# Paired one-hots, a moved register read and a moved seam between two expert layers

## The chip, the core and the metric

One NeuronCore of a Trainium2 chip runs the whole program. The metric is the device time of one execution in microseconds (us). The engines are TensorE (PE, with its weight loads as PEld), VectorE (DVE), ScalarE (ACT), GpSimd (POOL) and SyncE (SP), which here only issues transfers and reads registers for them. Each engine takes its instructions in order and waits at semaphores for the others.

## The reference

```python
# attention: (4, 8, 576, 64); heads 0-3 a window of 32, heads 4-7 a dilated one
x = attention(q, k, v)                # 2304 tokens x 512
def moe(x, w_gate, w1, w2, ...):      # twice, 8 experts, D=512, F=1024
    logits = x @ w_gate               # layer 2: + modality_bias[modality_id]
    e_idx = argmax(logits, axis=1)    # one expert for each token
    gate = softmax(logits)[e_idx]     # layer 1: times sigmoid(x @ w_output_gate)[e_idx]
    for e in range(8):
        out[e_idx == e] = gate * (relu(x[e_idx == e] @ w1[e]) @ w2[e])
```

The second layer takes the first one's output.

## The kernel before

All of it lies in one function, and the order of the instructions is written out by hand. The attention runs first (lines 283 to 656). Each expert layer then works on **slots** of 128 tokens, up to 27 of them (`NSLOT`), at least 18 (`NMIN`); from slot 18 on each lies in an `If` nested in the one before (L1019), and the number of slots `nsl` is read from the table `tab` into a register of every engine by `values_load` (L1018) behind slot 2 (`KE - 1`). Products are made in split 16-bit: a weight is a high part (`hi_piece`, L100, ScalarE) and a low part (`lo_piece`, L105, VectorE), both from the 32-bit `raw` that SyncE loads (L92) in eight pieces of 512 KB. `splits` takes a list such as `B8:12 D8:12`: split these pieces, then load the next expert's into their place.

A slot (`slot`, L946 on) gathers its tokens (POOL, L886), turns them (by DMA, L893, or on TensorE, L901), and makes two products. The first (`mm1`, L923) runs in two halves of 48 matmuls of 128 columns; each half ends in a relu by ScalarE (`hh`, L933) and its remainder by VectorE (`hl`, L934). The second (L997) has 24 matmuls of 512 columns, first over `hh`, the last eight over `hl`. Its result goes through `Post1.out` (ScalarE L1133, VectorE L1134) to 16-bit rows `y`, is written to DRAM, turned on TensorE (L1152) and by VectorE out of PSUM (L1153), and multiplied with the second router (`router`, L1161); VectorE adds the logits (L1170). The router's PSUM tile `plg` is a single one.

Other work is put between by **hooks**: `at(s, k, ...)` names a slot and a point in it. The points follow each other as 0 (ahead of the first half), 8 (behind 8 of its matmuls), 1 (behind 32), 2 (behind the half), then its relu, 3, 4 (behind 32 of the second half), the second relu, 5, then 9, 6, 10 (behind 4, 12, 20 matmuls of the second product) and 7 (behind it).

`sort` (L701 to 872) is such work, cut in steps: from the logits it makes each token's expert, by a scan and two matmuls its place, then two one-hots (its slot, `ob`, L806, L807; its row, `A`, L812), from which matmuls make the index (`pidx`, L817) and the gates (`pg`, L863). `table` makes `tab` and after it slot 3's weights are asked for. `first_slots` (L224 to 277) does the same for the two slots that a layer begins with: in the attention's tail for layer 1 and in slots 15 to 17 for layer 2. In slots 0 to 2 the first expert's weights serve; slot 3's are split by `FIRST[0]` to `FIRST[3]` from hook (1, 6) on. Slots 0 and 1 of layer 1 keep their results in PSUM (`pya`) until slot 2's hook (2, 5), where `first_out` brings them out; at (2, 7) they are turned.

The last slot of layer 1 has its rows made, turned and put through the router by layer 2's first hooks (`out(None)`, L1129, L1130; `router(None)`, L1167, L1168), and the sort of layer 2 (`so2`) begins behind that.

## Time and profile before

| | us |
|---|---|
| median of 3 runs (643.93 to 645.22) | 644.5 |
| the profiled execution | 644.33 |
| its span, first to last instruction | 642.6 |
| TensorE busy | 590.8 (92%) |
| VectorE busy | 366.6 (57%) |
| ScalarE busy | 272.9 (42%) |
| POOL busy | 191.4 (30%) |

The attention fills the first 152 us, layer 1 follows to 425 and layer 2 to 634. A matmul's end is modelled, so matmuls overlap in the records, and a busy share near one only says that TensorE was never seen idle. An idle time in brackets stands ahead of the instruction that ended it, with the engine or transfer whose signal came last. "issue" is time in which nothing visible was waited for. Register reads and branches are not counted as busy.

### The profile page before, as it was taken

To read this page: it belongs to the slowest core of one execution; us is meant where nothing else is said; L and a number is where in the kernel's file an instruction comes from. 1 tells how busy PE (TensorE), PEld (TensorE's weight loads), DVE (VectorE), ACT (ScalarE), POOL (GpSimd) and SP (SyncE) were. 2 spreads that over 40 slices of the span, in tenths; PEclk is the share of its full clock that TensorE was granted. 3 is DMA by queue.
4 is the path that set the end of the run, shared out by engine and by line. 5 is a ranking of instruction groups with operands and counts; after the bars stand their busy time and mean duration, and the time that the engine had idled before them with its cause. 6 is when DMAs were issued, how large, how long until landed. Compare 5 with 4: busy or idle time off the path is not lost. (4 is left out here: it accounts for less than half of the span.)

```text
span 642.6 us, 19352 instructions
## 1 busy us (share of the span) xinstructions
PE 590.8 (92%) x7380; PEld 456.6 (71%) x7380; DVE 366.6 (57%) x653; ACT 272.9 (42%) x370; POOL 191.4 (30%) x305
## 2 busy tenths in 40 slices
PE   3879788977989999999999999989999999999994
PEld 2768677977667767777686686866776777777772
DVE  6798888788888436953848922249541101013460
ACT  5767666772185115923626611111532111114550
POOL 2657767613132310001110410002553212212220
PEclk9889999866999999999999999999999999999998
DMA  8864759872399765995967872220994514133921
GB/s 285 258 202 165 232 173 298 268 160 71 119 378 328 226 119 151 357 298 140 236 222 205 204 165 56 57 32 18 307 331 135 103 51 101 53 99 95 306 63 37
DMA packets 100864, 114.15 MB, mean 178 GB/s; under 512 B 64399, under 2 KB 69263, under 8 KB 100752
## 3 DMA queue, kind: packets, MB, share of 16 engines
q1 hardware_dynamic: 95072, 94.89, 51.8%
q0 software_dynamic: 5280, 17.13, 8.7%
q8 instruction: 59, 0.97, 0.6%
q10 hardware_dynamic: 400, 0.72, 0.3%
q14 instruction: 53, 0.43, 0.2%
HBM read 209.13 MB, written 18.22 MB: 354 GB/s over the span
## 5 line engine op out<-in xcount | busy, mean ns | idle before, releaser
L923 PEld LDWEIGHTS <-wb 128*128 128x128 f16 x4032 | 229.4, 98 | 8.6 <-issue 3.6
L923 PE MATMUL ph<-xT,wb 128*128 128x128 f16 x3648 | 210.7, 219 | 2.2 <-DMA xT<-xg 1.1
L934 DVE SCALAR_TENSOR_TENSOR hl<-ph,hh 128x512 f16<-128x512 f32 x84 | 57.7, 689 | 164.3 <-ACTq L942 145.2
L997 PE MATMUL py<-wb,hh 128*128 128x512 f16 x608 | 137.9, 379 | 1.8 <-ACT hh L933 1.8
L997 PEld LDWEIGHTS <-hh 128*128 128x128 f16 x672 | 63.5, 98 | 71.5 <-ACT hh L933 2.7
L933 ACT ACTIVATE hh<-ph 128x512 f16<-128x512 f32 x84 | 50.2, 597 | 150.9 <-PE ph L923 145.3
L105 DVE SCALAR_TENSOR_TENSOR wb<-raw,wb 128x1024 f16<-128x1024 f32 (+1 forms) x80 | 104.6, 1346 | 13.2 <-ACT wb L100 11.8
L100 ACT ACTIVATE wb<-raw 128x1024 f16<-128x1024 f32 (+1 forms) x80 | 87.2, 1135 | 8.1 <-ACTq L942 4.1
L997 PE MATMUL py<-wb,hl 128*128 128x512 f16 x304 | 71.8, 379 | 0.0
L997 PEld LDWEIGHTS <-hl 128*128 128x128 f16 x336 | 32.8, 98 | 40.2 <-DVE hl L934 0.9
L1263 POOL DMA_INDIRECT out<-y,idx x16 | 16.2, 1011 | 99.0 <-ACTq L942 80.7
L447 PE MATMUL po<-v,pT 128*96 128x65 f32 x384 | 41.2, 260 | 0.1
L447 PEld LDWEIGHTS po<-v,pT 128*96 128x96 f32 x384 | 37.9, 176 | 0.2 <-DVE xh L454 0.2
L386 PE MATMUL ps<-kk,qs 128*96 128x128 f16 x192 | 30.4, 231 | 4.5 <-DVE qs L370 2.1
L886 POOL DMA_INDIRECT xg<-x_dram,idxaa x23 | 25.4, 1103 | 29.7 <-DMA xT<-xg 18.6
L386 PE MATMUL ps<-kk,ql 128*96 128x128 f16 x192 | 30.6, 232 | 3.7 <-DVE ql L364 3.7
L431 PE MATMUL pst<-mt,msel 128*128 128x96 bf16 x192 | 30.1, 217 | 4.0 <-ACT mt L420 4.0
L434 ACT ACTIVATE pT<-pst 128x384 f32<-128x384 f32 x48 | 23.5, 490 | 22.8 <-PE pst L433 22.1
L387 DVE TENSOR_REDUCE M<-ps 96x4 f32<-96x512 f32 x48 | 31.6, 681 | 2.6 <-PE ps L386 2.1
L1262 ACT ACTIVATE y<-py,gsb 128x512 f32<-128x512 f32 x16 | 11.0, 686 | 51.2 <-PE py L997 48.3
L386 PEld LDWEIGHTS <-ql 128*96 128x96 f16 x192 | 23.9, 132 | 12.2 <-DVE ql L364 5.4
L386 PEld LDWEIGHTS <-qs 128*96 128x96 f16 x192 | 24.2, 131 | 9.6 <-issue 4.1
(401 smaller groups left out, 727.7 us busy)
## 6 DMA issues: line engine op xcount, KB each, us to landing
raw<-in_w1a SPq DMA_DIRECT2D x95, 512.0 KB
raw<-in_w2a SPq DMA_DIRECT2D x92, 512.0 KB
raw<-in_w1b SPq DMA_DIRECT2D x75, 512.0 KB
raw<-in_w2b SPq DMA_DIRECT2D x72, 512.0 KB
qk<-in_qk SPq DMA_DIRECT2D x16, 608.0 KB
v<-in_vw SPq DMA_DIRECT2D x16, 390.0 KB
y_dram<-y SPq DMA_DIRECT2D x11, 260.0 KB
y_dram<-lotmp SPq DMA_DIRECT2D x10, 260.0 KB
```

Source lines behind the costliest of these rows:

```text
L100: nc.scalar.activation(wb[:, 0, s], raw[:, s], AF.Copy, scale=SW)
L105: nc.vector.scalar_tensor_tensor(out=wb[:, 1, s], in0=raw[:, s], scalar=SW, in1=wb[:, 0, s], op0=ALU.mult, op1=ALU.subtract)
L386: nc.tensor.matmul(ps[:, j, :], q[:, h, QT * i:QT * i + QT], kk[:, h, QT * i:QT * i + 128], start=False, stop=w == 1 and j == 3, skip_grou ...
L387: nc.vector.tensor_reduce(out=Ms[n][:, 4 * g:4 * g + 4], in_=ps, axis=AX.X, op=ALU.max)
L431: nc.tensor.matmul(ps[:, j, :], msel[:, typ, j, :], mt[:, g, :], start=j == 0, stop=False, skip_group_check=True)
L434: nc.scalar.activation(pTs[n][:, 4 * g:4 * g + 4, :], ps, AF.Exp, scale=0.125 / (SQK * SQK))
L447: nc.tensor.matmul(po[:, h, i, :], pT[:, NQ * h + i, :], v[:, h, i, :], start=True, stop=True)
L886: nc.gpsimd.indirect_dma_start(t, None, src, bass.IndirectOffsetOnAxis(start.idx[:, s:s + 1], 0))
L923: nc.tensor.matmul(ph[:, j, :], w[:, c, fs], xT[:, parts[c + i], :], start=k == 0, stop=k == 47, skip_group_check=True)
L933: nc.scalar.activation(hs, ph, AF.Relu)
L934: nc.vector.scalar_tensor_tensor(out=hl[:, 4 * g:4 * g + 4, :], in0=ph, scalar=0.0, in1=hs, op0=ALU.max, op1=ALU.subtract)
L997: nc.tensor.matmul(to, a, w, start=k == 0, stop=k == len(ops) - 1)
```

## The change

Six edits. (1) One-hots are compared in pairs: the index of each token is copied twice, side by side, as 16-bit values (`pp2`, `pr2`), and `one_hot` compares it with two neighbouring columns at a time; the slots' one-hots get a 28th column (`NSP`) so that their number is even, and all operands are 16-bit. (2) The sort keeps `eq` by expert, so that the 16-bit `oh` is written in a row instead of in strides; two passes read in strides instead. (3) The third and fourth split of slot 3's weights go behind the first half of slot 2 and behind its second. (4) The read of the number of slots goes from behind slot 2 to behind 20 matmuls of its second product. In slot 17 the router product of slot 15 goes from ahead of the second half to behind 4 matmuls of the second product. (5) In layer 2's slot 0 the turn of layer 1's last rows goes from ahead of the first half to behind 32 of its matmuls, router and sort's first step behind the half, the sort's second step behind 4 matmuls of the second product. (6) The hint ahead of each branch on `nsl` is also given to VectorE.

The allocations of `Bg`, `obp`, `pidx` and `pg` grow from `NSLOT` to `NSP` columns; their readers take the first 27.

```diff
@@
+NSP = 28
+HINT = [mybir.EngineType.PE, mybir.EngineType.DVE]
@@
-    tokv = const.tile([P, NSLOT], F16, name="tokv")
+    tokv2 = const.tile([P, NSLOT, 2], F16, name="tokv2")
+    tokv = tokv2[:, :, 0]
...
+    def one_hot(out, vals, pairs):
+        n, m = out.shape[1], out.shape[2] // 2
+        sh = [P, n, m, 2]
+        nc.vector.tensor_tensor(out.rearrange("p t (j k) -> p t j k", k=2),
+                                vals.rearrange("p (j k) -> p j k", k=2).unsqueeze(1).to_broadcast(sh),
+                                pairs.unsqueeze(2).to_broadcast(sh), op=ALU.is_equal)
@@ first_slots
+        pp2 = T("fp2", [-1, 2], F16)
+        v.tensor_copy(pp2, pi[:, 2].unsqueeze(2).to_broadcast([P, n, 2]))
...
-            v.tensor_tensor(A[:, a:e], iota_row.unsqueeze(1).to_broadcast([P, e - a, P]), pi[:, 2, a:e].unsqueeze(2).to_broadcast([P, e - a, P]), op=ALU.is_equal)
+            one_hot(A[:, a:e], iota_row, pp2[:, a:e])
@@ sort
-        eq = T("eq", [-1, E])
-        v.tensor_tensor(eq, lg, mxb, op=ALU.is_equal)
-        v.tensor_tensor(eq, eq, desc.unsqueeze(1).to_broadcast(sh), op=ALU.mult)
+        eq, st = T("eq", [E, -1]), [P, E, nt]
+        v.tensor_tensor(eq, lg.rearrange("p t e -> p e t"), mx.unsqueeze(1).to_broadcast(st), op=ALU.is_equal)
+        v.tensor_tensor(eq, eq, desc.unsqueeze(2).to_broadcast(st), op=ALU.mult)
         mi, mb = T("mi", [-1]), T("mb", [-1])
-        v.tensor_reduce(out=mi, in_=eq, axis=AX.X, op=ALU.max)
+        v.tensor_reduce(out=mi, in_=eq.rearrange("p e t -> p t e"), axis=AX.X, op=ALU.max)
...
-        v.tensor_tensor(oh.rearrange("p e t -> p t e"), eq, mb.unsqueeze(2).to_broadcast(sh), op=ALU.is_equal)
+        v.tensor_tensor(oh, eq, mb.unsqueeze(1).to_broadcast(st), op=ALU.is_equal)
...
+        bmh = T("bmh", [NSP], F16)
+        gp.memset(bmh[:, NSLOT:], 0.0)
         gp.tensor_scalar(bm, s_even, h, 1000.0, op0=ALU.is_ge, op1=ALU.mult)
-        gp.tensor_tensor(bm, bm, bs, op=ALU.add)
+        gp.tensor_tensor(bmh[:, :NSLOT], bm, bs, op=ALU.add)
...
+        pr2 = T("pr2", [2, -1, 2], F16)
+        v.tensor_copy(pr2, pi[:, 1:3].unsqueeze(3).to_broadcast([P, 2, nt, 2]))
...
-        v.tensor_tensor(ob, bm.unsqueeze(1).to_broadcast(sb), pi[:, 1].unsqueeze(2).to_broadcast(sb), op=ALU.is_equal)
-        v.tensor_tensor(obp, ob, tokv[:, :nt].unsqueeze(2).to_broadcast(sb), op=ALU.mult)
+        one_hot(ob, bmh, pr2[:, 0])
+        s4 = [P, nt, NSP // 2, 2]
+        v.tensor_tensor(obp.rearrange("p t (j k) -> p t j k", k=2), ob.rearrange("p t (j k) -> p t j k", k=2),
+                        tokv2[:, :nt].unsqueeze(2).to_broadcast(s4), op=ALU.mult)
...
-            v.tensor_tensor(A[:, a:a + n], iota_row.unsqueeze(1).to_broadcast([P, n, P]),
-                            pi[:, 2, a:a + n].unsqueeze(2).to_broadcast([P, n, P]), op=ALU.is_equal)
+            one_hot(A[:, a:a + n], iota_row, pr2[:, 1, a:a + n])
@@ slot
-                tc.mark_branch_hint_location(f"{start.name}{s + 1}", hint=nsl > s + 1, engines=PE)
+                tc.mark_branch_hint_location(f"{start.name}{s + 1}", hint=nsl > s + 1, engines=HINT)
...
-            if s == NMIN - 1:
-                post.router(s - 2)
...
                 if k == 4:
                     hook(9)
+                    if s == NMIN - 1:
+                        post.router(s - 2)
...
                 if k == 20:
                     hook(10)
+                    if s == KE - 1:
+                        count()
...
+        def count():
+            nonlocal nsl
+            nsl = nc.values_load(tab[0:1, 0, 31:32], min_val=1, max_val=NSLOT)
+
         for s in range(NMIN):
             slot(s, nsl)
-            if s == KE - 1:
-                nsl = nc.values_load(tab[0:1, 0, 31:32], min_val=1, max_val=NSLOT)
@@ plan of layer 1
-    at(2, 0, lambda: gt.memset(y16p[1][:, 2 * DM:], 0.0), lambda: start1.first_splits(FIRST[2]))
+    at(2, 0, lambda: gt.memset(y16p[1][:, 2 * DM:], 0.0))
     at(2, 1, lambda: start1.turned(KA + 1))
     at(2, 2, run(so1))
-    at(2, 3, lambda: start1.first_splits(FIRST[3]))
+    at(2, 3, lambda: start1.first_splits(FIRST[2]))
+    at(2, 5, lambda: start1.first_splits(FIRST[3]))
@@ plan of layer 2
-    at(0, 0, lambda: post1.out(None, py1), lambda: post1.transposes(None))
-    at(0, 8, lambda: post1.router(None), run(so2))
-    at(0, 5, run(so2))
+    at(0, 0, lambda: post1.out(None, py1))
+    at(0, 1, lambda: post1.transposes(None))
+    at(0, 2, lambda: post1.router(None), run(so2))
+    at(0, 9, run(so2))
```

## Rows read from the trace of the kernel before

**Rows 1.** Busy time by stage: start:end, length, each engine's busy us (count), clock, DMA share, GB/s.
```profile
180.00:200.00 20.00, 17.09 (x237) 13.69 (x235) 16.16 (x15) 14.96 (x17) 8.44 (x14) 1.00 1.05 358
...
197.00:213.50 16.50, 16.15 (x234) 13.20 (x232) 15.64 (x32) 6.57 (x9) 1.44 (x2) 1.00 1.05 356
...
340.00:370.00 30.00, 28.77 (x362) 20.92 (x360) 28.19 (x41) 19.91 (x24) 7.76 (x9) 1.00 0.74 203
...
420.00:460.00 40.00, 36.67 (x447) 26.76 (x445) 24.78 (x68) 7.78 (x12) 11.00 (x18) 1.00 0.28 91
460.00:634.00 174.00, 173.59 (x1963) 125.89 (x1961) 50.51 (x54) 53.42 (x72) 47.43 (x63) 1.00 0.48 137
```

**Rows 2.** Timeline of TensorE: start, length, operation, count, [idle before it <- what ended it].
```profile
163.05 1.90 PE L997 MATMUL pya<-wb,hl 128*128 128x512 f16 x8 [0.29 <-DVE hl L934]
...
167.31 0.59 PE L997 MATMUL pya<-wb,hh 128*128 128x512 f16 x2 [0.30 <-DVE wb L105]
...
182.72 1.27 PE L863 MATMUL pg<-Bga,Aa 128*128 128x135 f16 x18
...
188.05 1.90 PE L997 MATMUL py<-wb,hh 128*128 128x512 f16 x8 [1.38 <-ACT hh L933]
...
195.99 2.84 PE L923 MATMUL ph<-xT,wb 128*128 128x128 f16 x48 [1.14 <-DMA xT<-xg]
...
213.54 0.61 PE L1152 MATMUL pyt<-identh,y 128*128 128x128 f16 x8 [0.39 <-DVE fe_meb L196]
...
359.78 0.44 PE L1161 MATMUL plg<-wr2h,yT 128*128 128x8 f16 x12 [1.23 <-DVE lg L1170]
...
426.77 0.40 PE L1152 MATMUL pyt<-identh,y 128*128 128x128 f16 x4 [1.50 <-ACT y L1129]
```

**Rows 3.** Groups of VectorE's instructions by shape: count | busy us, mean ns | idle before.
```profile
L1153 DVE COPY yT<-pyt 128x1024 f16<-128x1024 f16 x22 | 15.0, 681 | 0.9 <-PE pyt L1152 0.9
...
L370 DVE COPY qs<-qs 64x1152 f16<-64x1152 f16 x15 | 6.8, 451 | 0.2
...
L812 DVE TENSOR_TENSOR Ab<-c16t,pib 128x1152 f16<-128x1152 f16 x3 | 3.9, 1352 | 0.0
...
L724 DVE TENSOR_TENSOR ohb<-eqb,mbb 128x216 f16<-128x216 f32 x1 | 1.1, 1128 | 0.0
...
L759 DVE TENSOR_REDUCE posb<-psb 128x27 f32<-128x216 f32 x1 | 0.5, 544 | 0.0
...
L718 DVE TENSOR_REDUCE mib<-eqb 128x27 f32<-128x216 f32 x1 | 0.4, 378 | 0.0
```

**Rows 4.** Timeline, the attention's last stage, VectorE behind the first one-hot.
```profile
144.53 0.17 DVE L451 TENSOR_SCALAR rc<-po 96x12 f32<-96x12 f32 x1 [0.74 <-PE po L447]
```

**Rows 5.** Timelines of ScalarE and of VectorE, slot 2 of layer 1.
```profile
184.51 1.91 ACT L100 ACTIVATE wb<-raw 128x2048 f16<-128x2048 f32 x1 [1.46 <-DMA raw<-in_w2a]
...
187.38 0.61 ACT L933 ACTIVATE hh<-ph 128x512 f16<-128x512 f32 x1
...
189.82 2.29 DVE L105 SCALAR_TENSOR_TENSOR wb<-raw,wb 128x2048 f16<-128x2048 f32 x1 [0.48 <-ACT wb L100]
...
193.29 0.74 DVE L1134 SCALAR_TENSOR_TENSOR xgA<-pya,gsa,xgA 128x512 f16<-128x512 f32 x1
```

**Rows 6.** Instructions of line 1018, TensorE's: ns min/median/max, first and last start us.
```profile
L1018 PEldq TENSOR_LOAD <-tab x2: 402/634/865, 195.1 to 461.8; - x2
```

**Rows 7.** Timeline of VectorE, slot 17 of layer 1.
```profile
364.79 3.52 DVE L105 SCALAR_TENSOR_TENSOR wb<-raw,wb 128x1024 f16<-128x1024 f32 x3
```

**Rows 8.** Timeline, ScalarE and VectorE where layer 2 begins.
```profile
426.03 0.69 ACT L1129 ACTIVATE y<-py,prg 128x512 f16<-128x512 f32 x1 [6.04 <-SPq L1019]
...
429.23 0.24 DVE L1167 TENSOR_TENSOR lgt<-plg,eqlaa 128x80 f32<-128x80 f32 x1 [0.55 <-PE plg L1161]
...
433.19 0.61 DVE L727 TENSOR_TENSOR_SCAN incb<-mask,ohb 128x216 f16<-128x216 f16 x1
...
441.44 3.89 DVE L812 TENSOR_TENSOR Ab<-c16t,pib 128x1152 f16<-128x1152 f16 x3
```

More of the change, by code (lines that the diff above doesn't have):

```diff
@@ L162, in slot_consts @@
         v.memset(s_odd[:, 1:2], 0.0)
-    tokv = const.tile([P, NSLOT], F16, name="tokv")
+    tokv2 = const.tile([P, NSLOT, 2], F16, name="tokv2")
+    tokv = tokv2[:, :, 0]
     def token_values():
-        nc.vector.tensor_scalar(tokv, blk128, iota_p, -TOK0, op0=ALU.add, op1=ALU.add)
+        nc.vector.tensor_scalar(tokv2, blk128.unsqueeze(2).to_broadcast([P, NSLOT, 2]), iota_p, -TOK0, op0=ALU.add, op1=ALU.add)
     zt = const.tile([P, ROW], F16, name="zt")
@@ L800, in table @@
             start.eql, start.nlast = eql, nlast
-        sb = [P, nt, NSLOT]
+        sb = [P, nt, NSP]
         nf = 3 + len(extra)
-        Bg = T("Bg", [-1, 1 + nf, NSLOT], F16)
-        ob, obp = Bg[:, :, 0], T("obp", [-1, NSLOT], F16)
-        v.tensor_tensor(ob, bm.unsqueeze(1).to_broadcast(sb), pi[:, 1].unsqueeze(2).to_broadcast(sb), op=ALU.is_equal)
-        v.tensor_tensor(obp, ob, tokv[:, :nt].unsqueeze(2).to_broadcast(sb), op=ALU.mult)
+        Bg = T("Bg", [-1, 1 + nf, NSP], F16)
+        ob, obp = Bg[:, :, 0], T("obp", [-1, NSP], F16)
+        one_hot(ob, bmh, pr2[:, 0])
+        s4 = [P, nt, NSP // 2, 2]
+        v.tensor_tensor(obp.rearrange("p t (j k) -> p t j k", k=2), ob.rearrange("p t (j k) -> p t j k", k=2),
+                        tokv2[:, :nt].unsqueeze(2).to_broadcast(s4), op=ALU.mult)
         yield
@@ L811, in sort @@
             n = min(ACH, nt - a)
-            v.tensor_tensor(A[:, a:a + n], iota_row.unsqueeze(1).to_broadcast([P, n, P]),
-                            pi[:, 2, a:a + n].unsqueeze(2).to_broadcast([P, n, P]), op=ALU.is_equal)
+            one_hot(A[:, a:a + n], iota_row, pr2[:, 1, a:a + n])
         yield
-        px = pp.tile([P, NSLOT], F32, name="pidx", tag="pyt")
+        px = pp.tile([P, NSP], F32, name="pidx", tag="pyt")
         for t in range(nt):
@@ L820, in sort @@
         idxf = T("idxf", [NSLOT])
-        v.tensor_scalar(idx, px, TOK0, None, op0=ALU.add)
-        act.activation(idxf, px, AF.Copy, bias=TOK0)
+        v.tensor_scalar(idx, px[:, :NSLOT], TOK0, None, op0=ALU.add)
+        act.activation(idxf, px[:, :NSLOT], AF.Copy, bias=TOK0)
         start.idx, start.idxf = idx, idxf
@@ L835, in sort @@
             so, sg = T("so", [-1, E]), T("sg", [-1])
-            v.tensor_tensor(so, eq, mi.unsqueeze(2).to_broadcast(sh), op=ALU.is_equal)
+            v.tensor_tensor(so, eq.rearrange("p e t -> p t e"), mi.unsqueeze(2).to_broadcast(sh), op=ALU.is_equal)
             v.tensor_tensor(so, og, so, op=ALU.mult)
@@ L859, in sort @@
         yield
-        pg = pp.tile([P, 1 + nf, NSLOT], F32, name="pg", tag="plg")
+        pg = pp.tile([P, 1 + nf, NSP], F32, name="pg", tag="plg")
         for t in range(nt):
@@ L864, in sort @@
         fl = m1.tile([P, 1 + nf, NSLOT], F32, name=f"fl{nm}")
-        act.copy(fl, pg)
+        act.copy(fl, pg[:, :, :NSLOT])
         g = m1.tile([P, NSLOT], F32, name=f"gs{nm}")
```

## The prediction

> **What bounds the kernel now.** I read the busy time by stage first, then TensorE's timeline with its gaps, then for each gap the engine that ended it. From 460 us to the end TensorE is busy for 173.59 of 174 us [rows 1]: nothing in that stretch can be won by moving work, it only starts earlier or later. The granted clock is 1.00 there and in all the stretches the change touches [rows 1]. So the change is worth what it takes out of the gaps, and those are few: about 3 us in 180 to 200, 1.2 us in 340 to 370, 3.3 us in 420 to 460 [rows 1]. Each has its place: in layer 1's slot 0 the second product waits for VectorE (0.29 and 0.30 us), in slot 2 for ScalarE (1.38), at the start of slot 3 (1.14), in slot 4 (0.39), in slot 17 (1.23), and at the seam of the layers (1.50 in its largest piece) [rows 2]. The second thing to see is VectorE: 28.19 of 30 us busy in 340 to 370 [rows 1]. Where it is that full, a TensorE gap that goes is replaced by a wait for VectorE, and the gain is VectorE's shift, not the gap's length.
>
> The profiled execution took 644.33 us (span 642.6, 1.7 around it), 0.17 under the median of 644.5. I sum against 644.33 and add 0.17 at the end.
>
> **One-hots in pairs.** Before, every one-hot is a product of a row with one element repeated; 1152 elements take 1352 ns [rows 3]. No row shows a two-source operation over 16-bit pairs, so its price is bounded: below by the copy of 1152 16-bit elements, 451 ns, above by the 1352 ns of now [rows 3]. I take the copy of 1024 16-bit elements out of PSUM, 681 ns, which cannot use the fastest form either: 681 x 1152/1024 = 0.77 us a piece, and at the same pace 0.50 us for the 756 elements of a slot one-hot in layer 2 and 0.34 for the 504 in layer 1 (before, at 1352/1152, 0.86 and 0.57). The Trainium skill's VectorE: DVE Perf Modes (What auto-detection actually checks) says that a two-source operation handles two elements a cycle if all its tensors are 16-bit with a step of 1; by its 0.96 GHz a piece would be 0.60 us plus the fixed part (estimate), so the sum would be the one I take; no run so far shows such an operation.
>
> The transposed one-hot of the sort writes 16-bit elements in strides and takes 1128 ns for 216; contiguous I price it like the contiguous pass over 216 elements, 378 ns [rows 3]. In exchange two passes now read in strides; the row of such a read is 544 against 378 ns [rows 3], so plus 0.17 each. Net for layer 2's sort: 1.13 - 0.38 - 0.34 = 0.41 us shorter; for layer 1's 144 elements two thirds, 0.3. Each sort also gets one small cast, some 0.2 us.
>
> In **slot 0 of layer 1** VectorE saves 0.3 - 0.2 + 2 x 0.23 (slot one-hots) + 2 x 0.58 (row one-hots) = 1.7 us before the index is out. TensorE's waits of 0.29 and 0.30 go, with a smaller one between; the index, the table and so the request for slot 3's weights come about 1.1 us earlier (0.6 to 1.3).
>
> The same one-hot in the attention's tail (1664 elements) saves nothing: the next VectorE operation waits 0.74 us for TensorE anyway [rows 4]. The 28th column adds 27 elements to a slot's products in layer 2, 0.03 us each at 1352/1152 ns an element, four or five of them per layer; they lie beside the big product's matmuls, and uncovered would cost 0.15 us.
>
> **The splits of slot 2.** Now ScalarE's third split sits ahead of the first relu: it waits 1.46 us for its weights at 184.51, runs 1.91, and the relu comes at 187.38 [rows 5]; TensorE's 1.38 us is that. After, the relu runs as soon as the copy of the 18 gate matmuls is out, which end at 184.0 now [rows 2] and 1 us earlier then, so at 183.5 to 184, and the split behind it: at 184.0 to 184.5, limited by its data, not later than now. So TensorE's second product starts when its first is done, 3 us earlier. But at its end it needs the two rows of results of slots 0 and 1, and those VectorE makes last: the fourth low split (189.82, 2.29 us), then y and y of slot 1, ending at 194.03 [rows 5]. In the new order VectorE does: first low part of hl at 184.5, third low split 185.9 to 188.2, second hl to 188.9, fourth low split to 191.2, the two y to 192.6: 1.4 us earlier than now, 0.95 if the weights came no earlier. Of the moved loads on SyncE's queue the first pair (2 x 512 KB) now goes behind the slot's transposing DMA instead of ahead of it and is issued with the third low split's end, within 0.5 us of now; the second pair with the fourth's, earlier. The transposing DMA itself no longer sits behind them.
>
> **The register read.** TensorE's read of the slot count takes 402 and 865 ns in the two layers [rows 6]. The long one is the 1.14 us gap in front of slot 3 [rows 2]. In layer 2 the short one, at 461.8, costs nothing: TensorE shows no gap there [rows 1], it works on the matmuls queued ahead of it. Four matmuls from the end of a product, with 12 or more of 0.2 us in the queue, the first is covered too; if that cover were gone the price is the gap it makes now. On VectorE, POOL, ScalarE and SyncE it is 0.3 to 0.5 us, ahead of work that waits longer for something else.
>
> **Layer 1's start in sum.** TensorE alone would reach slot 3 2.8 us earlier. VectorE, busy for all but a trace of 197 to 213.5 [rows 1], reaches its first split there 1.75 to 2.7 us earlier (its y 1.4, plus what the turn and the register reads no longer queue). In slot 4 TensorE already waits 0.39 us for it [rows 2], so VectorE's shift decides: -2.1 us, from -1.2 to -2.7. The transfers are at their limit there too (share 1.05 [rows 1]); each load is let go by a low split, so they shift with VectorE.
>
> **The router product.** At 359.78 TensorE waits 1.23 us because the bank of logits is single and its last reader, on VectorE, comes late [rows 2]. Moved into the second product, the router finds it free. But its own reader now stands behind the three splits at 364.79, which end at 368.3 [rows 7], and the next router product, at the slot's end, needs the bank again. VectorE is about 0.7 us earlier by then (two pieces of 640 elements and one of 384 at nearly half price, less one cast) and 0.3 by hl no longer waiting: 367.3. TensorE would be there at 367.1 (from 359.78 - 1.23 on, 3.1 for 48 matmuls and the transposes, 5.1 for 24 wide ones, 0.3 for the moved router). It waits some 0.4: gain 0.8, from 0 to 1.23.
>
> **The seam.** Now: y by ScalarE at 426.03, the transposes 1.50 us late, the copy, the router, then the sort from 429.23 to 433.80, and its first matmul follows at once, with no product of slot 0's second half done [rows 2, 8]. After, TensorE starts the first product as soon as its branch is through, about 425.95, as the other engines do now [rows 8]. 32 matmuls (2.84 us for 48, the last one's tail of some 0.15 off: 0.056 us apart [rows 2]) take it to 427.7; y is done at 427.5 and hides. Transposes, copy, router: 429.55, so the sort begins 0.3 later than now, is 0.41 shorter, and ends at 433.7. TensorE reaches the sort's matmuls after four of the second product at 432.95 and waits 0.85 us. By then it has done four matmuls (0.85 us) that it now does afterwards, and it goes on 0.15 us earlier: gain 1.0, from 0.6 to 1.4. The row one-hots (3.89 us from 441.44 [rows 8]) come to 2.3 and end 1.7 us ahead of the index matmuls, so they don't wait.
>
> **Hints for VectorE.** No row shows one on VectorE. In the late slots VectorE waits for TensorE most of the time (it is busy for 50.51 of 174 us in layer 2's [rows 1]), so the instructions themselves cost nothing. At the seam all engines go through the last branch between 425.27, where TensorE's wait of 1.50 us begins, and 426.03 [rows 2, 8]; if VectorE were the last one through, a branch fetched ahead could give back some of these 0.76 us, and if the hint fetched the wrong way it could cost as much. I take 0, the near end, since ScalarE's wait there was ended by SyncE's branch and not VectorE's [rows 8].
>
> **Sum.** 2.1 + 0.8 + 1.0 = 3.9 us: 644.33 - 3.9 + 0.17 = 640.6; I write 640.5.
>
> **Rivals.** (1) The pairs run at the old pace, so only reorderings count. Then the weights come no earlier (-1.2 us in layer 1), the router's reader is late (-0.1), and the row one-hots end after TensorE has reached the index matmuls, which eats all but 0.1 of the seam: 643.1. For it: no row shows the pair form; against: the copies of 16-bit data in rows 3. Chance 0.1. (2) VectorE's queue takes back one of the two smaller gains (the router's reader behind three splits, or the sort as the limit at the seam): 641.5. For it: VectorE is full at both places. Chance 0.14. (3) Slower: runs of two elements are handled like the strided 16-bit write of 1128 ns for 216 elements, 5.2 ns each. Then a piece of 1152 takes 6 us, three of them in layer 2 alone hold the index matmuls by some 15 us, and the kernel ends above 660. It turns slower than before from about 2.2 us a piece (1.9 ns an element). Against: all three operands are adjacent in memory two by two, and the output fully. Chance 0.04. (4) The forecast, 0.7. The rest, 0.02, is a stall of another kind.
>
> **How the numbers follow.** All gains at their upper bounds, 2.7 + 1.23 + 1.4, give 639.2 and with the hint 638.5; (2) with layer 1 at its lower bound gives 642.5. I set 638.7 to 642.7; (1) and (3) are left out. A difference of 0.2%, 1.3 us, is about what can be told from no change: faster ends below 643.2. Of (1) half falls within 0.2%. Faster 0.87, same 0.08, slower 0.05.
>
> **What would show it.** Row one-hots of 0.7 to 0.8 us for 1152 elements; no gap ahead of slot 2's second product, but 1 to 1.6 us ahead of the transposes at its end; no register read in a gap; in slot 4 a wait of about 1 us for VectorE; in slot 17 no gap before the second half and less than 0.5 ahead of the last router; at the seam one gap of 0.6 to 1 us ahead of the sort's matmuls. Wrong would be: pieces at 1.35 us; new gaps marked as issue; or splits in slots 3 to 5 that wait for weights.

## The result

The changed kernel took 637.69 us (median of 6 runs, 635.75 to 638.38), the kernel before 644.21 in the runs beside it: a ratio of 0.9899, 95% interval 0.9878 to 0.9920, so 6.5 us less (5.2 to 7.9). In two more measurements beside the kernel before, further down, the ratio was 0.9906 (0.9886 to 0.9927) and 0.9923 (0.9903 to 0.9943): 5.3 and 5.5 us between the medians (6.1 and 5.0 by the ratios). Forecast were 640.5 us and so a gain of 3.7. The direction was right, the gain too small, and the first measured median lies 1.0 us below the range of 638.7 to 642.7 (the two later ones, 638.86 and 638.84, at its lower edge). That is not one error of size: a gain was overlooked in the attention, one at the start of layer 1 was put too low, and one at the seam did not come, because a cost priced at nothing, the branch hint on VectorE, stood in its place.

The profiled execution took 638.38 us. From its page: the span, and TensorE and VectorE (busy us, share of the span, instructions).

```profile
span 636.6 us, 19375 instructions
...
PE 589.1 (93%) x7380; PEld 456.1 (72%) x7380; DVE 359.9 (57%) x657; ACT 272.8 (43%) x370; POOL 196.1 (31%) x307
```

VectorE has 6.7 us less to do than before; TensorE still bounds the kernel. TensorE's waits in the changed kernel, from its timeline (start, length, operation, in brackets the wait ahead of it and what ended it; only lines with such a wait):

```profile
187.72 1.02 PE L1012 MATMUL py<-wb,hl 128*128 128x512 f16 x4 [0.42 <-issue]
...
189.67 0.40 PE L1174 MATMUL pyt<-identh,y 128*128 128x128 f16 x4 [0.70 <-DVE y L1156]
...
208.07 0.61 PE L1174 MATMUL pyt<-identh,y 128*128 128x128 f16 x8 [0.29 <-DVE fe_meb L199]
...
362.14 0.44 PE L1183 MATMUL plg<-wr2h,yT 128*128 128x8 f16 x12 [0.86 <-DVE lg L1192]
...
419.86 1.96 PE L940 MATMUL ph<-xsA,wb 128*128 128x128 f16 x32 [0.72 <-DVEq L1041]
...
423.21 0.40 PE L1174 MATMUL pyt<-identh,y 128*128 128x128 f16 x4 [1.17 <-DVE y L1152]
...
429.10 0.18 PE L743 MATMUL ct<-incb,c16t 128*128 128x8 f16 x1 [0.69 <-DVE incb L739]
```

Against [rows 2]: the two waits of slot 0 (0.29 and 0.30) and the one of 1.38 ahead of slot 2's second product are gone. (That of slot 0 ahead of `hl` is not gone for good: two later profiles of the changed kernel have one of 0.62 and 0.63 us there.) In slot 2 now stand 0.42 in the product and 0.70 ahead of the transposes; in slot 4 0.29 instead of 0.39; in slot 17 0.86, further back, instead of 1.23; at the seam 0.72, 1.17 and 0.69 instead of 1.50 and two small ones. One more shows in no line of this kind: `before` stands still in slot 1 of layer 1 for 0.87 us in small pieces (its 96 matmuls of the first product take 6.23 us, here 5.36), and 0.4 in slot 15. Its largest piece in `before`, in which TensorE waits for nothing that the profile shows ("issue"):

```profile
171.85 2.28 PE L923 MATMUL ph<-xsA,wb 128*128 128x128 f16 x38 [0.40 <-issue]
```

Whether it belongs to the code, the repeated profiles say.

The lengths below are taken from TensorE's records, from the first matmul of one slot to that of the next, in four profiles of the kernel before and three of the changed one (the first of each is the one shown here, the others come with the experiments). The attention's line is the time between two of VectorE's reductions at 35 to 42 us.

| us | before | after | difference of means | forecast |
|---|---|---|---|---|
| attention, the stretch at 35 to 42 us | 6.69 6.69 6.68 6.68 | 5.73 5.72 5.73 | -0.96 | none |
| layer 1, slots 0 to 4 | 66.86 65.67 66.29 66.37 | 63.45 62.59 62.65 | -3.4 (-3.0 without slot 1's stall) | -2.1 |
| slot 17 | 12.98 13.40 13.52 13.09 | 12.72 12.53 12.58 | -0.64 | -0.8 |
| seam: last second product of layer 1 to the end of layer 2's second slot | 32.65 33.86 32.64 34.28 | 33.06 33.11 33.14 | -0.26 (+0.46 against the first and third) | -1.0 |
| both layers, first to last matmul | 481.02 480.83 480.99 481.87 | 477.12 476.13 476.28 | -4.67 | -3.9 |

Attention and layers together make 5.6 us, which agrees with the 5.3 and 5.5 of the two later measurements and lies in the interval of the first. Where layer 1 begins is no part of the table: it lies between 150.56 and 152.61 us in the four profiles of before and between 149.60 and 152.18 in the three of after, so the total of a single profile says little.

### The profile page after: what moved, and what is told of

It reads as the page before. It is cut to its first block, busy times and chain, and to the rows that moved or that the text cites. A ratio compares the mean times of both kernels' runs of the same rounds, so it can differ in the third digit from the quotient of the medians.

```text
span 636.6 us, 19375 instructions
## 1 busy us (share of the span) xinstructions
PE 589.1 (93%) x7380; PEld 456.1 (72%) x7380; DVE 359.9 (57%) x657; ACT 272.8 (43%) x370; POOL 196.1 (31%) x307
```

## The experiments

In each series all kernels ran on one chip, beside runs of the kernel before.

**Repeating both kernels.** The two profiles compared above differ in places that the change doesn't touch.

> The kernel before, unchanged, profiled once more. In its first profile TensorE begins layer 1 at 152.61 us, and it stands still without a visible reason for 0.87 us in slot 1 (around 171.5) and 0.4 us in slot 15 (around 338). Theory A (these belong to the execution, not to the code): layer 1 begins somewhere else, by 1 us or more, and at least one of the two stalls is gone or elsewhere; from slot 2 to slot 15 the distances between slots agree with the first profile to 0.1 us apart from such stalls. Theory B (they belong to the code of before): start of layer 1 within 0.3 us of 152.61 and both stalls in the same place and of the same size.

> The changed kernel, unchanged, profiled and timed once more. Theory A (a part of the measured 6.5 us is chance: the clock in the attention and stalls of TensorE's queue): ratio to before nearer to 0.993 than to 0.990, layer 1 begins later than the 150.56 us of its first profile. Theory B (all of it is the change): ratio 0.988 to 0.992 again. Both: VectorE's first instruction behind the last branch of layer 1 comes about 2.1 us behind the branch, as in the first profile.

Measured: the profiled execution of before 642.75 us; the medians 644.15 for before and 638.86 for after (ratio 0.9906). Neither before nor after had the stall of slot 1, and before lost as much elsewhere: at the seam its granted clock fell, and the stretch took 33.86 instead of 32.65. So the stall is no property of the code of before, and the table's gain from the first pair of profiles contains it. Theory A held for the stall; that layer 1 of the changed kernel begins later (152.18 against 150.56) held as well, but the ratio came nearer to B's. Of slots 2 to 15 of before two differ by more than the 0.1 us expected: slot 2 took 16.26 instead of 16.40, slot 4 11.61 instead of 11.84.

> The kernel before, unchanged, profiled a third time. In the first profile TensorE's queue stood still for 0.87 us in slot 1 and 0.4 us in slot 15 of layer 1 at full clock at the seam; in the second both stalls were absent, but the granted clock fell to 0.5 behind the waits at the seam (0.66 in 425 to 430), and layer 2's first product took 1.2 us longer. Theory A (both are matters of the execution, each present in a part of the runs, and the changed kernel, with shorter waits at the seam, shows neither): one of the two is there again. Theory B (they are rare and the profiles caught them by luck): neither. Layers (first matmul of layer 1 to the last matmul) under A 480.5 to 482.3 us, under B about 479.6.

Measured: 642.26 us, the stall is there again (slot 1 takes 11.82 us, without it 10.98; slot 15 11.76, without it 11.34), and the clock at the seam stays up. A last pair, in a series with other kernels:

> The kernel before, unchanged, on the chip that the next three run on. TensorE's queue stood still for 0.87 us in slot 1 in all seven traces of two chips and in none of four traces of a third, whatever the kernel. Theory A (the stall goes with the chip): it is there in all four kernels of this call or in none. Theory B (it goes with the code): here yes, in the changed kernel no.

> The changed kernel on the same chip. Theory A (stall by chip; then the change is worth what the traces give stage by stage: 0.96 in the attention, 2.6 at layer 1's start, 0.6 in slot 17, 0.2 at the seam or 1.4 where the clock would have fallen, so 4.4 to 5.6): 4.4 to 5.6 us below before. Theory B (6.5 us as first measured): 6 us or more below before.

Measured: the profiled execution of before 644.69 us; the medians 638.84 for after and 644.36 for before, 5.5 us apart (ratio 0.9923), inside theory A's band. No kernel of that series has the stall. Over the later profiles: it is in all seven of two series and in none of the eight of two others, whatever the kernel. (The first pair, before with it and after without, stands outside of this count: whether the two belong to one series is not known.) But one of the series with and one without ran on the same chip, so it goes with the series, not with the code and not with the chip. Its cause stays open. Where it was absent, the kernel before had the fallen clock at the seam (both times; where the stall was there, none of five with the old seam). So each of the four profiles of before loses time by one of the two, 1.3 us by the stall or 1.2 to 1.6 by the clock. Only the second is a loss that the change removes: a kernel with the whole of the new order, further down, has the stall. The seam of before_fourth and of after_third, in stretches of 3 us (busy us and count of TensorE, its loads, VectorE, ScalarE, POOL; then the granted clock, DMA share, GB/s):

```profile
424.00:427.00 3.00, 1.11 (x16) 0.90 (x16) 1.20 (x3) 0.69 (x1) 0.18 (x1) 1.00 0.02 5
427.00:430.00 3.00, 2.66 (x38) 2.53 (x36) 2.28 (x7) 0.00 (x0) 1.02 (x1) 0.66 0.23 89
430.00:433.00 3.00, 3.00 (x45) 3.00 (x43) 2.79 (x7) 0.60 (x1) 0.00 (x0) 0.77 0.00 0
```

```profile
418.00:421.00 3.00, 2.17 (x36) 1.99 (x36) 0.40 (x1) 0.69 (x1) 0.06 (x1) 1.00 0.03 8
421.00:424.00 3.00, 2.59 (x52) 2.53 (x53) 1.89 (x5) 0.60 (x1) 1.01 (x1) 1.00 0.09 36
424.00:427.00 3.00, 2.61 (x36) 1.88 (x33) 2.69 (x9) 0.60 (x1) 0.00 (x0) 1.00 0.16 58
```

In before TensorE is busy for 1.11 of the 3 us ahead of the fall and then runs at a granted 0.66 and 0.77 over two stretches, partly at its lower level of 1.2 GHz: the stretch is 1.6 us longer than in the first profile (34.28 against 32.65). In after it is busy for 2.17 and 2.59 and stays at 1.00. So the seam's new order has a second worth that [rows 1] could not show: it spares a fall that only some executions of before have. In two of seven profiles with the old order the clock falls there, in none of ten with the new one.

**The hint.** One edit against the changed kernel:

```diff
-HINT = [mybir.EngineType.PE, mybir.EngineType.DVE]
+HINT = [mybir.EngineType.PE]
```

> The changed kernel, with the branch hint given to TensorE alone, as before. Theory A (the hint makes VectorE wait 2.14 us for its code behind the branch that leaves layer 1, where the kernel before waits 0.15): that wait falls to about 0.15 us, the transposes of the last row start at 421.7 instead of 423.2 and the wait of 0.69 us ahead of the sort's matmuls goes: the seam gains 1.9 us, the time falls 1.2 to 1.9 us under that of the changed kernel. Rival B (VectorE's wait comes from the new order at the seam or from where the code lies, and the hint has no part in it): the 2.1 us stay and the time is that of the changed kernel within 0.3 us.

Measured: 636.28 us (ratio 0.9876, 0.9853 to 0.9900), 2.6 below the changed kernel of the same series, more than the 1.2 to 1.9 expected. VectorE around the branch that leaves layer 1, first in the changed kernel, then with the hint for TensorE alone:

```profile
419.17 0.17 DVE L1192 SCALAR_TENSOR_TENSOR lg<-plg,lg 128x8 f32<-128x8 f32 x1 [3.99 <-PE plg L1183]
422.40 0.75 DVE L1152 SCALAR_TENSOR_TENSOR y<-py,prg,y 128x512 f16<-128x512 f32 x1 [3.07 <-issue]
```

```profile
417.91 0.17 DVE L1192 SCALAR_TENSOR_TENSOR lg<-plg,lg 128x8 f32<-128x8 f32 x1 [3.99 <-PE plg L1183]
419.37 0.75 DVE L1152 SCALAR_TENSOR_TENSOR y<-py,prg,y 128x512 f16<-128x512 f32 x1 [1.30 <-ACT y L1151]
```

With the hint VectorE begins its half of the last row 3.07 us after the logits' addition and waits for nothing that the profile shows ("issue"); without, 1.30 us after, and then it is ScalarE's half that it waits for. In the records the next instruction comes 2.14 us behind the branch with the hint (2.18 and 2.21 in the later profiles) and 0.15 without. Behind each of the five branches before, where the next slot does follow, it comes at once in both. Behind the branch that leaves layer 2, which has the hint too, it comes after 0.16 us. TensorE, at the seam with the hint for TensorE alone:

```profile
418.54 1.96 PE L940 MATMUL ph<-xsA,wb 128*128 128x128 f16 x32 [0.67 <-DVEq L1041]
...
426.44 0.18 PE L743 MATMUL ct<-incb,c16t 128*128 128x8 f16 x1 [0.69 <-DVE incb L739]
```

The wait of 1.17 us ahead of the transposes is gone, the stretch takes 31.67 us, that is 0.98 less than 32.65. The wait of 0.69 ahead of the sort's matmul stayed, against the expectation: counted from layer 2's first matmul the sort begins 1.3 us earlier, and TensorE reaches that matmul as much earlier. The Trainium skill, Runtime: NRT & Kernel Launch (Instruction fetch mechanics), says that a branch to code outside of what was fetched in sequence costs a fetch; it gives no time for it and says nothing of hints. That the hint fetched the slot's code and not what lies behind the last one would fit layer 1, but the 0.16 us at layer 2's end do not fit it; shown is only that the wait at the seam comes and goes with the hint. Repeated in the last series:

> The changed kernel with the branch hint for TensorE alone, on the same chip as the changed kernel. VectorE's 2.1 us behind the branch cost 1.4 to 1.5 us in the layers of the traces on the first chip; theory A: 1.2 to 1.8 us below the changed kernel; rival: below 0.5 us, the first difference was chance.

Measured: 636.83 us against 638.84, 2.0 less (1.2 to 1.8 expected). In TensorE's records the hint costs 1.4 us at the seam in both pairs (33.11 and 33.14 against 31.67); the rest of the 2.6 and 2.0 stands in no stage.

**One element at a time.**

```diff
-        nc.vector.tensor_tensor(out.rearrange("p t (j k) -> p t j k", k=2),
-                                vals.rearrange("p (j k) -> p j k", k=2).unsqueeze(1).to_broadcast(sh),
-                                pairs.unsqueeze(2).to_broadcast(sh), op=ALU.is_equal)
+        sh = [P, out.shape[1], out.shape[2]]
+        nc.vector.tensor_tensor(out, vals.unsqueeze(1).to_broadcast(sh), pairs[:, :, 0:1].to_broadcast(sh), op=ALU.is_equal)
```

and the same for the product with `tokv`.

> The changed kernel, whose one-hots compare one element at a time again (same 16-bit operands, same 28 columns). Theory A (the pairs bring VectorE forward, and that is most of what layer 1's start gained): a row one-hot of 1152 elements takes 1.3 us instead of 0.74, the index matmuls of slot 0 wait again for about 0.3 us or more, slot 3 begins 0.6 to 1.2 us later in relation to slot 0, and layer 2's index matmuls wait up to 1 us: time 1 to 2 us above the changed kernel. Rival B (the reordering alone gives the gain, VectorE has room): below 0.4 us. Rival C (the 16-bit row is what is fast, pairs or not): the pieces stay at about 0.75 us and nothing moves.

Measured: 641.37 us, 2.5 above the changed kernel of the same series. One-hots and some neighbours in the changed kernel, by shape (count, busy us and mean ns), and then with one element at a time:

```profile
L230 DVE TENSOR_TENSOR Ab<-c16t,pr2b 128x1152 f16<-128x1152 f16 x3 | 2.1, 752 | 0.0
...
L230 DVE TENSOR_TENSOR Bgb<-bmhb,pr2b 128x756 f16<-128x756 f16 x1 | 0.6, 552 | 0.1
L730 DVE TENSOR_REDUCE mib<-eqb 128x27 f32<-128x216 f32 x1 | 0.5, 548 | 0.0
...
L736 DVE TENSOR_TENSOR ohb<-eqb,mbb 128x216 f16<-128x216 f32 x1 | 0.4, 384 | 0.0
...
L783 DVE CAST pr2b<-pib 128x108 f16<-128x108 int32 x1 | 0.2, 217 | 0.0
```

```profile
L229 DVE TENSOR_TENSOR Ab<-c16t,pr2b 128x1152 f16<-128x1152 f16 x3 | 3.9, 1350 | 0.0
...
L229 DVE TENSOR_TENSOR Bgb<-bmhb,pr2b 128x756 f16<-128x756 f16 x1 | 0.9, 945 | 0.1
```

752 against 1350 ns for the same 1152 16-bit elements: the pairs are what is fast, not the 16-bit row (rival C falls). By TensorE's records slot 0 gets 0.8 to 1.3 us longer, slot 2 0.1 to 0.6, slot 17 0.4 to 0.6 and layer 2's second slot 0.7: above the 1 to 2 us expected, since slot 17 and slot 2 were not counted.

**The seam alone and the splits alone, on the kernel before.**

> The kernel before with the new order at the seam alone (hint to TensorE only, old one-hots, sort and split order). Theory A (the seam's new order is worth 1.0 us as forecast, and more where it also spares the fall of the clock): the stretch from the last slot of layer 1 to layer 2's third slot takes 31.8 to 32.3 us (before: 32.65 and, with the clock down, 33.86), with one wait of 1.0 to 1.3 us ahead of the sort's matmuls since the sort is not shortened here; granted clock 1.00 all through it; time 0.6 to 1.8 us below before. Rival B (the row one-hots of 1.3 us hold the index matmuls and eat the gain): 32.6 us or more, and no gain in time.

Measured: 643.52 us, ratio 0.9990 (0.9969 to 1.0012), no difference that can be told, against the 0.6 to 1.8 us expected. The stretch takes 32.44 us: 0.2 less than before without a fall of the clock, between A's band and B's. The wait is as expected:

```profile
431.87 0.18 PE L731 MATMUL ct<-incb,c16t 128*128 128x8 f16 x1 [1.20 <-DVE incb L727]
```

and the rest goes in layer 2's second slot, 0.27 longer, where the index comes later. So the new order without the shorter sort and one-hots is worth 0.2 us; with them it is 1.0.

> The kernel before with the third and fourth split of slot 3's weights moved behind slot 2's two halves, and nothing else (the count is read behind slot 2 as before). Theory A (VectorE decides at slot 2's end): ScalarE's wait of 1.4 to 1.6 us ahead of the second product is gone, and a new wait of 1 us or more stands ahead of the transposes at its end; slot 2 takes 15.2 to 15.7 us (16.40 and 16.26 before). Rival B (ScalarE was the bound and the whole wait is gained): 14.6 to 14.9 us. Rival C (the splits now come too late for slot 3): slot 2 as in A, but splits or relus of slot 3 or 4 hold TensorE and give it back.

Measured: slot 2 takes 15.30 us. Both waits for ScalarE's relu are gone. TensorE waits in a new place, ahead of the transposes, and ahead of slot 3 as it did before ([rows 2]):

```profile
191.81 0.40 PE L1152 MATMUL pyt<-identh,y 128*128 128x128 f16 x4 [0.65 <-DVE y L1134]
...
193.98 2.84 PE L923 MATMUL ph<-xT,wb 128*128 128x128 f16 x48 [1.12 <-DMA raw<-in_w2a]
```

0.65 us ahead of the transposes, for VectorE's result, and 1.12 ahead of slot 3, where the register is read (1.14 in the first profile of before, 0.81 in the third). The waits are those of theory A, the new one smaller than its 1 us. The length of slot 2 doesn't decide: 15.30 lies in A's band, but the same code as in before took 16.40, 16.26, 15.76 and 16.67 us in its four profiles, 15.62 in the kernel with the new seam, and 15.03 and 16.08 in two later ones. Beside the two kernels of the same series with the old order (15.76 and 15.62) slot 2 gains 0.3 to 0.5 us, and slot 4 0.5 (11.31 against 11.84); slots 0 to 4 together are 0.9 us shorter than in either. One profile of the edit is too little for more than this: the splits alone give about the 0.95 us that were forecast for weights that come no earlier, and nothing of it is lost in slots 3 and 4.

**What the forecast overlooked.** In the attention `token_values` writes `tokv`, and the change makes it write the values twice; of these lines the diff above shows only the tile:

```diff
-        nc.vector.tensor_scalar(tokv, blk128, iota_p, -TOK0, op0=ALU.add, op1=ALU.add)
+        nc.vector.tensor_scalar(tokv2, blk128.unsqueeze(2).to_broadcast([P, NSLOT, 2]), iota_p, -TOK0, op0=ALU.add, op1=ALU.add)
```

> The kernel before with one thing of the change alone: the token values are written twice, side by side (tokv2), by one VectorE instruction in the attention; its readers take the first of each pair. In all five profiles of kernels with the old tile that instruction (27 elements) takes 1.22 us and stands beside a POOL operation that ends with it, in all five with the new one 0.27 us. Theory A (the new form does not wait for POOL; the prediction missed this): 0.27 us, TensorE's wait behind it falls from 1.92 to 0.96 us, the granted clock stays at 1.00 between 40 and 48 us, layer 1 begins 0.95 us earlier at equal clock, the layers are as before, and the time is 0.6 to 1.6 us below before. Rival B (what differs between the two groups of profiles there comes from something else in the code): 1.22 us again, and no gain.

Measured: 643.00 us, ratio 0.9973 (0.9957 to 0.9989), so 0.7 to 2.8 us less by one instruction (0.6 to 1.6 expected). VectorE and POOL in the kernel before (its second profile), then with this edit alone:

```profile
38.47 1.67 DVE L158 TENSOR_SCALAR slots<-slots 128x27 f32<-128x27 f32 x1
...
40.27 1.22 DVE L167 TENSOR_SCALAR tokv<-cft 128x27 f16<-128x27 f32 x1
```

```profile
38.46 1.64 POOL L469 TENSOR_TENSOR x<-xh,x 96x768 f16<-96x768 f32 x1
40.18 1.27 POOL L366 TENSOR_TENSOR ql<-qk,qs 64x576 f16<-64x576 f32 x1
```

```profile
38.49 1.67 DVE L158 TENSOR_SCALAR slots<-slots 128x27 f32<-128x27 f32 x1
...
40.29 0.27 DVE L168 TENSOR_SCALAR tokv<-cft 128x54 f16<-128x54 f32 x1
```

```profile
38.48 1.64 POOL L470 TENSOR_TENSOR x<-xh,x 96x768 f16<-96x768 f32 x1
40.20 1.27 POOL L367 TENSOR_TENSOR ql<-qk,qs 64x576 f16<-64x576 f32 x1
```

In the kernel before both of VectorE's operations last until POOL's beside them has ended: 38.47 + 1.67 and 38.46 + 1.64; 40.27 + 1.22 and 40.18 + 1.27. With the values written from a repeated source the second takes 0.27 us beside the same POOL operation. TensorE's wait behind it, before and with the edit, and the stretches around it (columns as above):

```profile
42.14 0.38 PE L382 MATMUL ps<-mS,identb 96*96 96x512 bf16 x1 [1.92 <-DVE M L387]
```

```profile
41.20 0.38 PE L383 MATMUL ps<-mS,identb 96*96 96x512 bf16 x1 [0.96 <-DVE M L388]
```

```profile
40.00:44.00 4.00, 2.08 (x36) 1.91 (x33) 3.93 (x11) 1.32 (x3) 1.38 (x2) 0.92 0.71 196
44.00:48.00 4.00, 3.96 (x36) 3.49 (x33) 3.82 (x7) 3.08 (x5) 2.05 (x6) 0.66 0.64 152
```

```profile
40.00:44.00 4.00, 2.96 (x49) 2.64 (x47) 3.90 (x13) 2.25 (x5) 1.40 (x2) 1.00 0.68 194
44.00:48.00 4.00, 2.81 (x33) 2.11 (x32) 3.60 (x6) 2.56 (x5) 2.98 (x7) 1.00 0.63 135
```

The wait falls from 1.92 to 0.96 us, and the fall of the clock behind it (0.92 and 0.66 here; in all six profiles with the old `tokv` it lies between 41 and 48 us, in none of the eleven with the new one) doesn't happen. The Trainium skill, SBUF — State Buffer (Who interferes with whom), says that a one-source operation of VectorE in a fast two-port form and an operation of POOL shut each other out for their whole length; the trace agrees for the old form, which ends with POOL's operation both times. That the new form escapes it is shown by the run alone. A second edit tried the same for the operation ahead of it, by writing it with two sources:

```diff
-        v.tensor_scalar(s_even, s_even, -1.0, None, op0=ALU.add)
+        v.scalar_tensor_tensor(out=s_even, in0=s_even, scalar=-1.0, in1=zt[:, 0:NSLOT], op0=ALU.add, op1=ALU.add)
```

> As the kernel with the new token values alone, and the instruction of 27 elements that comes three ahead of it (the slots' constants minus one, 1.67 us beside a POOL operation of 1.64 us that ends with it) written as an operation with two sources instead of one. Theory A (one-source operations of VectorE that run at a higher rate wait for POOL's; other forms don't): about 0.2 us instead of 1.67, TensorE's wait there falls below 0.3 us, the stretch gets 0.7 to 1.5 us shorter. Rival B (whatever VectorE runs beside POOL at that place waits for it): still 1.6 us.

> The reordered kernel with the same instruction written with two sources. Theory A: 0.7 to 1.5 us below the reordered kernel, by the shorter wait in the attention at about 41 us. Rival B (as above): the same time as the reordered kernel.

Measured: theory A fell. The operation with two sources waits as long, again beside POOL's:

```profile
38.83 1.68 DVE L158 SCALAR_TENSOR_TENSOR slots<-slots,zt 128x27 f32<-128x27 f32 x1
38.82 1.64 POOL L470 TENSOR_TENSOR x<-xh,x 96x768 f16<-96x768 f32 x1
```

The first kernel took 642.32 us in its one run, the second 635.78 (ratio 0.9867), no different from the kernel without this edit in other series (0.9865 and 0.9851, next section). The same section of the Trainium skill says of an operation with two sources in SBUF that it contends with an operation of POOL that reads SBUF; the trace agrees (1.68 us beside 1.64).

**A better order.** Three moves on top of the hint for TensorE alone:

```diff
@@ plan of layer 2
-    at(0, 9, run(so2))
+    at(0, 6, run(so2))
@@ slot
             hook(5)
+            if s == NMIN - 1:
+                post.router(s - 2)
             sp(2)
...
                 if k == 4:
                     hook(9)
-                    if s == NMIN - 1:
-                        post.router(s - 2)
@@ plan of layer 1
-    at(2, 5, lambda: start1.first_splits(FIRST[3]))
...
     at(2, 5, first_out(post1, start1, 0))
-    at(2, 6, first_out(post1, start1, 1))
+    at(2, 5, first_out(post1, start1, 1))
+    at(2, 5, lambda: start1.first_splits(FIRST[3]))
```

> The changed kernel with four edits: hint to TensorE alone; the sort's second step behind 12 instead of 4 matmuls of layer 2's first second-product; slot 17's moved router ahead of the three splits and of the second product instead of 4 matmuls into it; the results of slots 0 and 1 brought out ahead of the fourth split instead of behind it. Theory A (VectorE's queue order makes the three waits left): the wait of 0.69 us ahead of the sort's matmuls, that of 0.5 to 0.9 us ahead of slot 17's last router and that of 0.7 us ahead of the transposes at slot 2's end go, and nothing else moves: 1.4 to 2.1 us below the kernel with the hint given back (636.28). Rival B (VectorE or the transfers are full there, and each wait comes back in the next slot): slots 3 to 5 get longer by as much as slot 2 gets shorter, and the gain is at most 1.2 us.

> The reordered kernel (hint, sort step, router, order of the splits and the results) on the same chip. In its trace slot 2 is 1.8 us shorter than in the kernel with the hint alone, slots 3 to 5 0.9 us longer, slot 17 0.8 and slot 23 0.9 shorter: 2.5 us in all, but on another chip its time was the same. Theory A (the times were those of different chips): 1.8 to 3.0 us below the kernel with the hint alone. Rival B (the gain does not reach the end): within 0.7 us of it.

Measured: first 636.42 us (0.9865, 0.9841 to 0.9889), no different from the 636.28 of the hint alone, which had run on another chip and in a series without the stall. Side by side in the last series 634.73 (0.9851, 0.9830 to 0.9872) against 636.83: 2.1 us less, inside theory A's band, and 4.1 less than the changed kernel. TensorE's waits from 170 to 460 us in the first of the two profiles:

```profile
202.14 0.18 PE L195 MATMUL pfe<-fe_cntb,c16t 128*128 128x8 f16 x1 [0.55 <-DVE fe_cntb L192]
...
208.09 0.61 PE L1174 MATMUL pyt<-identh,y 128*128 128x128 f16 x8 [0.40 <-DVE fe_meb L199]
...
419.02 1.96 PE L940 MATMUL ph<-xsA,wb 128*128 128x128 f16 x32 [0.68 <-DVEq L1041]
...
443.52 2.84 PE L940 MATMUL ph<-xT,wb 128*128 128x128 f16 x48 [1.10 <-ACT xT L919]
```

The waits at slot 2's end, in slot 17 and ahead of the sort's matmul are gone. A part comes back: slots 3 to 5 take 35.60 instead of 34.64 us, because the fourth split and all that follows it on VectorE is later (the waits of 0.55 and 0.40). Against the hint alone slot 17 gains 0.8 us and layer 2's slot 0 0.9 in both series. Slot 2 does not repeat: it took 12.99 us in the first and 14.50 in the last series, where 0.36 and 0.82 us of waiting stood in it, no less than in the changed kernel. So the stages of the last pair give only 0.6 us (both layers 474.41 against 475.03), and the rest of the 2.1 between the medians isn't shown by them. At the seam 0.68 us at the branch remain; the 1.10 ahead of layer 2's third slot stand in every kernel.

## Why the prediction was right and wrong

**What bounds the kernel** held. The late slots take the same 10.54 us in both kernels, and the gaps of slot 2, slot 17 and the seam were replaced by waits for VectorE: 0.70, 0.86 and 0.69; in slot 4 0.29 of 0.39 us stayed.

**One-hots** held. 0.75 us a piece against 0.77; 0.38 for the transposed one-hot, 0.55 for the strided reads, 0.22 for the cast, all as priced from [rows 3]. The slots' one-hots took 0.55 and 0.42 instead of 0.50 and 0.34: the share of an instruction that doesn't shrink with its elements was left out. It was left out on both sides (before, 0.92 and 0.67 and not 0.86 and 0.57), so the saving came out as forecast. Rivals 1 and 3 are out.

**The attention** is the first step that failed: it stood at nothing, since the sum has no term for the instruction that writes `tokv`. That instruction stands at 40 us, far from the gaps that the forecast went through, and its new form was worth 0.96 us. What the clock adds that no longer falls behind it can't be told: layer 1 begins at 150.5 us in the mean of the eleven profiles with the new tile and at 151.4 in that of the six with the old one, 0.9 apart.

**Layer 1's start** had the mechanism and not the size: forecast -2.1, measured -3.0 (-2.5 in the first pair of profiles, and -2.5 with the three more kernels that begin layer 1 as before does and the two with the hint alone, always without slot 1's stall). Executions of one code differ by up to 0.9 us here, so the size of the miss is open between 0.4 and 0.9. Three steps of it were right in kind: no wait ahead of slot 2's second product; instead a wait for VectorE at its end, of 0.70 us (0.66 and 0.74 in the later profiles) and not 1 to 1.6; VectorE's results of slots 0 and 1 1.7 us earlier, counted from slot 0 (1.4 forecast). The step that failed is VectorE's shift of 1.75 to 2.7 us, which was to decide in slots 3 and 4. From VectorE's timeline, the changed kernel, then the line of before that answers to its last:

```profile
186.39 2.56 DVE L107 SCALAR_TENSOR_TENSOR wb<-raw,wb 128x2048 f16<-128x2048 f32 x1
...
189.53 0.74 DVE L1156 SCALAR_TENSOR_TENSOR xgA<-pya,gsa,xgA 128x512 f16<-128x512 f32 x1
...
191.39 2.34 DVE L107 SCALAR_TENSOR_TENSOR wb<-raw,wb 128x1024 f16<-128x1024 f32 x2
```

```profile
196.84 2.36 DVE L105 SCALAR_TENSOR_TENSOR wb<-raw,wb 128x1024 f16<-128x1024 f32 x2 [1.10 <-ACT wb L100]
```

VectorE's first split of slot 3 follows the copies without a wait, 40.83 us after slot 0's start; before it came 44.23 after, behind a wait of 1.10 for ScalarE's split. That is 3.4 us, as much as the 3.3 by which TensorE reaches slot 3 earlier in these two profiles (the stall of 0.87 is in both numbers). In the two later pairs, without the stall, it is 3.1 against 3.2 and 3.7 against 3.7. So VectorE keeps up with TensorE, which in slot 4 waits 0.29 and not 1 us, and TensorE's own 2.8 us, as the forecast has them, come through (2.9 in the mean, without the stall). The shift of VectorE was summed from its own operations; the wait for ScalarE's split, 1.10 us here and 0.53 to 0.85 in the later profiles of before, was not among them, and in the three profiles of after it is gone.

**The register read** is not always hidden: in the first profile of after it stops the product for 0.42 us although 20 wide matmuls stand ahead of it, with the hint for TensorE alone for 0.41 and 0.50, and in the two later profiles of after not at all. The cover named was the wrong one. What it costs is open: TensorE waits for VectorE right behind it with the stop (0.70 to 0.76 us) and without (0.66 and 0.74), and slot 2 takes 14.75 to 14.88 us with it, 14.28 and 14.50 without.

**The router** held: -0.64 against -0.8, with 0.86, 0.52 and 0.73 us ahead of the last one instead of "some 0.4". Its reader stands where it was put, behind three splits:

```profile
358.30 3.48 DVE L107 SCALAR_TENSOR_TENSOR wb<-raw,wb 128x1024 f16<-128x1024 f32 x3
361.92 0.17 DVE L1192 SCALAR_TENSOR_TENSOR lg<-plg,lg 128x8 f32<-128x8 f32 x1
```

**The seam** was right in every step but one. With the hint taken back it gains 0.98 us against 1.0 forecast. The hint was priced at 0 with 0.76 as the bound on both sides, and cost 1.4 us. The bound was the failing step: it took the time that all engines spend at the last branch without a hint on VectorE for the most that one with it could cost. No row showed a hint on VectorE, and for such an edit the rival that it does harm should have had a price of its own. Rival 2 (one of the smaller gains is taken back) named the loss, but by the sort, not by the branch. That the gain came out larger than forecast in spite of this loss is luck: the attention's 0.96 us and the clock's fall at the seam, neither of them in the sum, more than made up for it.

**The rest.** Of the first measured 6.5 us the stages give 5.6, and of these some 0.7 us come from executions of before in which the clock fell at the seam and some 0.6 from those with the stall in slots 1 and 15. The remaining 0.9 us are inside the interval; no stage shows them, and they stay open. With the term in the attention alone the forecast would have been 639.5.

## What to carry to other kernels

Cost every instruction whose operands an edit changes, also where it lies far from the edit's aim: look at what else runs beside it, above all on POOL. A gap on the bounding engine is worth what the next engine in line can give, and that engine's shift includes the waits that it loses, not only its own shorter work. An edit that no row can price, such as a branch hint on one more engine, should be tried by itself before it goes in with others: here it cost 2.0 of the 7.5 us between the medians that the rest gains.

## What the runs showed of the hardware

- A 27-element addition on VectorE takes 1.22 or 1.67 us beside an operation of POOL and ends with it; the same addition from a repeated source takes 0.27 us beside it.
- A branch hint on VectorE brought 2.14 us (2.18 and 2.21 in two more profiles) ahead of the first instruction behind the branch that leaves layer 1, against 0.15 without it; at the branch that leaves layer 2, hinted too, it was 0.16.
- One-hots of 1152 16-bit elements took 752 ns compared in pairs and 1350 ns one element at a time.
- TensorE's queue can stand still for 0.7 to 0.9 us in one slot in all kernels of one series of runs and in none of the next, on the same chip.
- Waits of 1.92 us in the attention, and of 1.50 and 0.39 at the seam, were followed by a fall of the granted clock, the first in all six profiles that have it, the second in two of seven; with 0.96 us there, in eleven profiles, and with single waits of at most 1.24 us here, in ten, it stayed at 1.00.
